# Pooled attention and a two-layer feed-forward network on one core: third and fourth pair in two visits, row maximum and scale in one instruction, new layouts for P and q, and a new order

## The chip, the cores and the metric

The kernel runs on one core of a Trainium2 chip. A core has five engines, each with its own queue in order: TensorE (PE; its weight loads are listed as PEld), VectorE (DVE), ScalarE (ACT), GpSimd (POOL) and SyncE (SP), which only issues DMA transfers. The metric is the device time of one execution in microseconds (us). Before the change it is 815.9 us, the median of three runs (814.71 to 816.48 us).

## The reference

Only what is computed matters here:

```python
def _attn_ref(q, k, v):                      # (4, 8, 1152, 64) fp32; q and k drawn about 0.71 wide, v 0.1
    q_pool = q.reshape(B, H, S // 2, 2, D).mean(axis=3)
    scores = (1 / np.sqrt(D)) * np.matmul(q_pool, k.transpose(0, 1, 3, 2))
    scores = scores - np.max(scores, axis=-1, keepdims=True)
    attn = np.exp(scores)
    attn = attn / (np.sum(attn, axis=-1, keepdims=True) + 1e-09)
    return np.matmul(attn, v)

def _moe_ref(x, w_in, w_out):                # x (2304, 512), w_in (512, 2048), w_out (2048, 512)
    r = np.maximum(x @ w_in, 0.0)
    return (r * r) @ w_out
```

`x` is the attention's output with the heads side by side: 2304 tokens of 512.

## The kernel before

**Attention.** The 32 heads of the four batches form 16 pairs, each of two heads of one batch. A pair has nine chunks of 128 pooled queries: four of head 0, four of head 1 and one that holds the last 64 queries of both. So there are 144 chunks. A chunk's scores (S, 128x1152, `scores`, L696 and L691) go to one of two PSUM tiles `s`; DVE takes the row maximum (MX, L704), ScalarE makes the Exp's bias from it (L715) and runs the Exp (EX, L716), which also gives the row sum. The scores of chunk i+2 need the Exp of chunk i, since they use its PSUM tile. Matmuls are in fp16, with each operand split in a high and a low part; for P that is HI (L720, L724, L353) and LO (L728), after which a DMA transpose (TR, L731) puts both into `PT`. The first four pairs are different: their P stays fp32 and is transposed by TensorE (TP, L756; copied out by TC, L766 and L768), and PV runs in fp32 (L867). PV (L875 for the other twelve pairs) runs twice a visit, r=0 on the first four 64-query columns of both heads and r=1 on the rest. For r=1 its moving operand has 384 columns, of which 64 are the other head's.

**Feed-forward.** Blocks of 256 tokens: block j takes r = j % 2 of the four pairs of batch j // 2, and a ninth block takes the 64 left over of every batch. A block is normalised with the row sums (RV, RT, RU, RB, XR), scaled by its own norm (XQ, XN, XM, XW) and split into high (XA, ScalarE) and low (XD, DVE). Then come eight H steps (L1025, 24 matmuls each), relu and square (HA, G1, G2, G3), and eight O steps (L1074, 12 matmuls each). Block 0 can start when its chunks of pairs 0 to 3 are done and the weights are ready.

**Weights.** Both matrices are loaded in 16 pieces as fp32 bits. Each value is taken apart and put together again in a range that can be split without loss: W1 (L1135, L353) scales, W2 (L1141, L1144) takes the sign, W3 (L1151) shifts by three bits, W5 (L1155) puts the three lowest bits in, W4 (L1164) multiplies by the sign. Then each quarter is scaled to high (WA, L328) and, for the second matrix, to a scaled fp32 copy (WB, L1241, ScalarE) and a low part (WD, L1245, POOL).

**What sets the order.** The kernel adds each step as an operation with the engines that may run it, an estimated cost, what it depends on, and a priority: its chunk number plus an offset for its kind (`off`, and `off0` before the first block) from the table `CFG`. `Plan.order` walks through these by estimated time and writes each engine's list; the engines then run their lists in order. Buffers come from seven tiles `buf`; `PT` has seven slots of 128 queries, and a chunk may write its slot when the PV that read it last is done (`ring`).

Of the kernel before, what the change touches and what calls it, by code (L numbers as in the profile page):

```python
# [8 lines left out]
F32 = mybir.dt.float32  # L9
# [3 lines left out]
I16 = mybir.dt.int16  # L13
AF = mybir.ActivationFunctionType
# [18 lines left out]
}  # L33


class Clock:


    W = 3413.3
# [12 lines left out]
    def run(self, t0, left):  # L52
# [3 lines left out]
        while True:  # L56
# [5 lines left out]
            self.used += self.edge - t  # L62
            left -= can
            t = self.edge
            self.turn()


class Plan:


    ENG = ("PE", "ACT", "DVE", "POOL", "SP")
    LAT = {"PE": 230, "ACT": 135, "DVE": 160, "POOL": 130, "SP": 150}

# [150 lines left out]
def kernel(  # L224
# [95 lines left out]
    def buf(*key):  # L320
        return bufs[plan.slot[key][1]]
# [1031 lines left out]
```

## Time and profile before

| | |
|---|---|
| median of three runs | 815.9 us |
| the profiled execution's own time | 815.77 us |
| its span, first to last instruction | 814.0 us |
| TensorE busy | 754.8 us (93%), mean granted clock 0.978 |
| ScalarE busy | 601.9 us (74%) |
| DVE busy | 585.2 us (72%) |
| POOL busy | 374.6 us (46%) |
| DMA, share of 16 engines | 76.7% in the queue of the kernel's own transfers |

Busy time is the time in which an engine runs an instruction; the share is of the span. A mean over the span says little here, since the program has stretches with different limits: the first four pairs with the weights, then attention and feed-forward blocks side by side, then blocks alone. A time line gives each instruction's start, and in square brackets how long its engine sat idle before it and what released it.

### The profile page before, as it was taken

The numbers are of one execution on the slowest core, as the hardware profiler recorded it, in microseconds if no ns is written. First come the engines' busy times: TensorE is split into PE (matmuls) and PEld (weight loads), VectorE is DVE, ScalarE is ACT, GpSimd is POOL, SyncE is SP. The second block draws the span as 40 slices with busy tenths as digits, with TensorE's granted clock in tenths as the row PEclk, the third lists the DMA queues.
The fourth block names the chain that finished last, engine by engine and source line by source line (L and its number), as shares of the span: only waits on it lengthen the run. The fifth ranks groups of instructions, "written<-read, shape, count | busy, mean of one in ns | idle before, by whom it ended". The sixth has DMA issues, their size and how long they took to land.

```text
span 814.0 us, 15284 instructions
## 1 busy us (share of the span) xinstructions
PE 754.8 (93%) x5998; PEld 493.6 (61%) x5998; DVE 585.2 (72%) x747; ACT 601.9 (74%) x940; POOL 374.6 (46%) x257
## 2 busy tenths in 40 slices
PE   5789888987799998999999999999999999999997
PEld 4555545554576656557756765677657656776663
DVE  3798898878997897689788897889678683311210
ACT  4676798899988688788898897998889974524230
POOL 2426333346867655657556684477655410000000
PEclk9899999997899999999999999999999999999999
DMA  9897645227689999999999999999999993000001
GB/s 280 210 238 233 150 155 162 102 47 167 131 177 207 192 213 198 211 193 198 204 216 192 206 200 195 198 213 154 211 197 197 173 169 63 1 14 14 14 14 26
DMA packets 324776, 128.96 MB, mean 158 GB/s; under 512 B 307552, under 2 KB 307552, under 8 KB 324704
## 3 DMA queue, kind: packets, MB, share of 16 engines
q1 hardware_dynamic: 324704, 127.99, 76.7%
q8 instruction: 47, 0.77, 0.4%
q14 instruction: 25, 0.20, 0.1%
HBM read 45.09 MB, written 4.72 MB: 61 GB/s over the span
## 4 chain that ended last, share of the span: by engine, by line
PE 61%; DVE 10%; DMA 9%; ACT 8%; issue 5%; POOL 4%; SPq 2%; POOLq 0%; DVEq 0%; ACTq 0%
PE ba L1074 14%; PE ba L1025 10%; PE ba L875 9%; PE s L696 8%; PE bt L1025 6%; PE bt L1074 5%; DMA PT<-buf 3%; ACT buf L716 3%; PE ba L867 3%; PE ba L756 2%; DVE ca L704 2%; DMA raw<-in_q_dram 2%; POOL buf L728 2%; DVE buf L728 2%; PE s L691 1%
## 5 line engine op out<-in xcount | busy, mean ns | idle before, releaser
L704 DVE TENSOR_REDUCE ca<-s 128x1 f32<-128x1152 f32 x144 | 193.1, 1350 | 20.2 <-PE s L696 16.2
L1025 PEld LDWEIGHTS <-w 128*128 128x128 f16 x1728 | 167.3, 98 | 31.1 <-issue 4.5
L716 ACT ACTIVATE buf<-s,ca,esc 128x1152 f32<-128x1152 f32 x135 | 177.0, 1311 | 8.1 <-DMA PT<-buf 2.0
L728 POOL TENSOR_TENSOR buf<-buf,buf 128x1152 f16<-128x1152 f32 x59 | 150.6, 2555 | 52.9 <-ACT buf L720 40.8
L1074 PE MATMUL ba<-w,region 128*128 128x512 f16 x672 | 153.7, 379 | 0.1
L696 PE MATMUL s<-kT,qT 128*128 128x512 f16 x720 | 137.3, 329 | 6.2 <-ACT buf L716 6.1
L1074 PEld LDWEIGHTS <-region 128*128 128x128 f16 x864 | 82.3, 98 | 93.1 <-issue 2.1
L1025 PE MATMUL ba<-region,w 128*128 128x256 f16 x1104 | 127.3, 273 | 2.9 <-DVE region L1037 2.5
L1052 POOL TENSOR_TENSOR region<-region 128x512 f16<-128x512 f32 x44 | 60.8, 1384 | 99.5 <-ACT region L1045 99.1
L696 PEld LDWEIGHTS <-qT 128*128 128x128 f16 x720 | 63.7, 100 | 62.8 <-issue 14.5
L875 PE MATMUL ba<-PT,v 128*64 128x384 f16 (+1 forms) x1296 | 95.0, 300 | 5.6 <-DMA PT<-buf 4.9
L728 DVE TENSOR_TENSOR buf<-buf,buf 128x1152 f16<-128x1152 f32 x49 | 78.3, 1597 | 20.2 <-ACT buf L720 11.1
L720 ACT ACTIVATE buf<-buf 128x1152 f16<-128x1152 f32 x75 | 87.0, 1161 | 5.8 <-DMA PT<-buf 2.1
L875 PEld LDWEIGHTS <-v 128*64 128x64 f16 x1296 | 73.7, 110 | 25.8 <-issue 8.2
L756 PE MATMUL ba<-ident,buf 128*128 128x128 f32 x324 | 55.2, 302 | 20.5 <-ACT buf L716 12.0
L715 ACT ACTIVATE ca<-ca,cols,esc 128x1 f32<-128x1 f32 x135 | 50.9, 377 | 19.1 <-DVE ca L704 18.4
L1040 ACT ACTIVATE region<-region 128x512 f16<-128x512 f32 x72 | 45.0, 626 | 21.1 <-PE ba L1074 8.1
L356 DVE SCALAR_TENSOR_TENSOR buf<-raw,psc,buf 128x576 f16<-128x576 f32 x45 | 55.5, 1260 | 5.9 <-POOL buf L330 3.5
L756 PEld LDWEIGHTS ba<-ident,buf 128*128 128x128 f32 x324 | 38.0, 152 | 35.5 <-ACT buf L716 13.2
L1052 DVE TENSOR_TENSOR region<-region 128x512 f16<-128x512 f32 x28 | 24.2, 866 | 47.8 <-ACT region L1045 47.4
L433 POOL TENSOR_TENSOR raw<-raw 128x576 f32<-128x576 f32 x16 | 24.2, 1515 | 61.2 <-DMA raw<-in_q_dram 44.0
L766 ACT ACTIVATE PT<-ba 128x384 f32<-128x384 f32 x74 | 34.0, 487 | 23.2 <-PE ba L756 21.2
(166 smaller groups left out, 961.0 us busy)
## 6 DMA issues: line engine op xcount, KB each, us to landing
raw<-in_k_dram SPq DMA_DIRECT2D x16, 576.0 KB, 4.6
raw<-in_q_dram SPq DMA_DIRECT2D x32, 288.0 KB, 4.8
region<-in_moe_w_in_dram SPq DMA_DIRECT2D x8, 1024.0 KB, 7.5
region<-in_moe_w_out_dram SPq DMA_DIRECT2D x8, 1024.0 KB, 5.2
raw<-in_v_dram SPq DMA_DIRECT2D x12, 576.0 KB, 4.5
out_dram<-buf SPq DMA_DIRECT2D x36, 128.0 KB, 2.4
v<-in_v_dram SPq DMA_DIRECT2D x4, 576.0 KB, 5.4
PT<-buf SPq DMA_TRANSPOSE x108, 4.9
```

The source lines that it names most:

```text
L356: nc.vector.scalar_tensor_tensor(out=o, in0=x, scalar=s, in1=h, op0=ALU.mult, op1=ALU.subtract)
L696: nc.tensor.matmul(s[:, x, :w], lhsT=qt[:, l, h, c0 : c0 + 2, :].rearrange("p a b -> p (a b)"), rhs=rhs, **st)
L704: nc.vector.reduce_max(a[:, 0:1], st3(), axis=AX.X)
L715: nc.scalar.activation(a[:, 1:2], a[:, 0:1], AF.Identity, bias=ln14, scale=s0)
L716: nc.scalar.activation(P(), st3(), AF.Exp, bias=a[:, 1:2], scale=s1, accum_out=col)
L720: nc.scalar.activation(hl()[:, 0], P(), AF.Copy)
L728: e.tensor_tensor(out=hl()[:, 1], in0=P(), in1=hl()[:, 0], op=ALU.subtract)
L756: nc.tensor.matmul(t[:, y], lhsT=P()[:, c * 128 : (c + 1) * 128], rhs=ident, is_transpose=True, start=(y == 0), stop=(y == 2), skip_group_ ...
L875: nc.tensor.matmul(px[h * 64 : (h + 1) * 64, :N], lhsT=vv[:, h, kc, vl, :], rhs=p2(r, h, 9 * pl + kc, False), start=(i == 0), stop=(i == 3 ...
L1025: nc.tensor.matmul(ph[:, f2], lhsT=w16[0][:, SLOT[f // 4], wl, a, f % 4 * 128 : (f % 4 + 1) * 128], rhs=xhl()[:, xl, a], start=(i == 0), s ...
L1052: e.tensor_tensor(out=gt[u][:, 1], in0=rt[u % 2], in1=gt[u][:, 0], op=ALU.subtract)
L1074: nc.tensor.matmul(p[:, :DM], lhsT=g[:, gl, f % 2, tt * 128 : (tt + 1) * 128], rhs=w16[1][:, SLOT[f // 4], wl, f % 4], start=(f == 0 and g ...
```

## The change

1. **Order of the first chunks.** The third and fourth pair are visited twice: first chunks 0, 1, 7, 8 of both (which block 0 needs), then the five others of both. Block 0's chunks are complete after 26 chunks and not after 31.
2. **Row maximum.** MX multiplies the scores by minus the scale, writes them back to the same PSUM tile, and takes the minimum into its accumulator output, all in one DVE instruction. The Exp then runs with the constant scale -1, and the minimum is its bias. For the fp32 chunks (pairs 0 to 3) there is no bias step; the others add a constant in a step of their own (MB), which may run on DVE, POOL or ScalarE. MX now needs the scale (GE) first.
3. **P's layout.** `PT` has the seven slots side by side for each block of 128 keys, so that PV reads one closed range: 256 columns for r=0 and 320 for r=1, where it was 384. The target of a DMA transpose now has a step of 896 elements between its 128-element pieces. `ringof` works out which PV has to be done before a slot is written; the first chunks behind the fp32 pairs wait for the last fp32 PV.
4. **q's layout.** The two heads' pooled queries lie in alternate partitions when loaded, so that one DMA transpose takes both; the scores read their weights with a step of two.
5. **Weights.** The three low bits are taken by an instruction of their own (W0, POOL or ScalarE) from the 16-bit half of the value, and the shift becomes the first operation of W5, so W3 goes.
6. **Smaller things.** GE, XO and the sum of q's halves (QS) may run on DVE; a half-width buffer `half` is added; v of an fp32 pair is loaded once; the factor 2^14 of the fp32 pairs moves from the Exp's bias to the row sums.
7. **Order.** `CFG`'s offsets and slacks are all new, and steps of the first and the last blocks get offsets of their own (`cls`).

ScalarE, behind the 36th Exp of the program (`L716`, first row). `w_1` is the second weight matrix; `L328` makes its high part and `L1241` its scaled copy:

```order
174 L716 ACTIVATE buf_93,sums_86<-s_112,ca,esc 128x1152
175 L766 ACTIVATE PT<-ba_113 128x384 x3
176 L715 ACTIVATE ca<-ca,cols,esc 128x1
177 L716 ACTIVATE buf_98,sums_87<-s_111,ca,esc 128x1152
178 L328 ACTIVATE w_1_91<-w_1_91,wS_1517 128x2048
179 L766 ACTIVATE PT<-ba_113 128x384
180 L766 ACTIVATE PT<-ba_114 128x384
181 L1241 ACTIVATE w_1_91<-w_1_91,wS_1517 128x2048
```

ScalarE of the changed kernel, around its 29th Exp (`L761`, first row), where the first of these now stands (`L338` high part, `L1306` copy):

```order
131 L761 ACTIVATE buf_93,sums_89<-s_112,ca 128x1152
132 L338 ACTIVATE w_1_91<-w_1_91,wS_1286 128x2048
133 L810 ACTIVATE PT<-ba_115 128x3x128
134 L810 ACTIVATE PT<-ba_114 128x3x128
135 L1306 ACTIVATE w_1_91<-w_1_91,wS_1286 128x2048
```

The pairs of weight instructions that stood behind the 37th Exp begin behind the 29th Exp; the last of them (row 155) is ahead of the 36th (row 158). No bias step (`L715`) stands between these rows.

ScalarE of the changed kernel behind its 36th Exp (first row); `L338` on `buf_97` is the high part of block 0's input, `L765` the high part of P, `L747` the bias step:

```order
158 L761 ACTIVATE buf_99,sums_86<-s_113,ca 128x1152
159 L761 ACTIVATE buf_98,sums_87<-s_112,ca 128x1152
160 L338 ACTIVATE buf_97<-x_110,xs 128x1024
161 L765 ACTIVATE buf_94<-buf_98 128x1152
162 L981 ACTIVATE ru<-ba_114 32x128
163 L810 ACTIVATE PT<-ba_115 128x3x128
164 L563 ACTIVATE half_100,acc<-raw_101 128x576
165 L810 ACTIVATE PT<-ba_114 128x3x128
166 L747 ACTIVATE ca<-ca,cols 128x1
167 L761 ACTIVATE buf_93,sums_87<-s_113,ca 128x1152
```

Block 0's input is split here, where the kernel before had weight instructions.

DVE before, at the low half of block 0's input (`L356` on `buf_94`), DVE's last step before the first H; the row maximum behind it (`L704`) is the 44th:

```order
242 L332 TENSOR_SCALAR region<-ba_113,esc 128x256
243 L993 RECIPROCAL xs<-xs 128x1
244 L356 SCALAR_TENSOR_TENSOR buf_94<-x_109,xs,buf_94 128x1024
245 L704 TENSOR_REDUCE ca<-s_112 128x1
246 L356 SCALAR_TENSOR_TENSOR region<-region,xs 128x1024
```

DVE of the changed kernel at the same step (`L369` on `buf_97`); the row maximum behind it (`L742`) is the 38th:

```order
203 L973 TENSOR_TENSOR r_1578<-ba_114,r_1578 128x16
204 L812 COPY PT<-ba_115 128x3x128
205 L369 SCALAR_TENSOR_TENSOR buf_97<-x_110,xs,buf_97 128x1024
206 L742 TENSOR_SCALAR s_113,ca<-s_113,esc 128x1152
207 L584 TENSOR_SCALAR ba_115<-ba_115 128x2
```

The step has moved ahead by six row maxima.

```diff
-CFG = {'SPLIT': 0, 'TURN': [], 'TURNB': [], 'WDP': ((1, 0), (1, 1), (1, 2), (1, 3)), 'WSP': 1.1562, ...
+CFG = {'SPLIT': 0, 'TURN': [], 'TURNB': [], 'WDP': ((1, 0), (1, 1), (1, 2), (1, 3)), 'WSP': 3.7027, ... 'PART': 1}
...
-    bufs = [buf_p.tile([128, 2304], F16, name=f"buf{i}") for i in range(NBUF)]
+    bufs = {
+        "buf": [buf_p.tile([128, 2304], F16, name=f"buf{i}") for i in range(NBUF)],
+        "half": [buf_p.tile([128, 1152], F16, name="half0")],
+    }
...
-    PT = pt_p.tile([128, 7, 18, 128], F16, name="PT")
+    PT = pt_p.tile([128, 18, 7, 128], F16, name="PT")
...
-    PSLOT = {0: 1, 1: 2, 7: 0, 8: 3, 2: 4, 3: 5, 5: 0, 6: 3, 4: 6}
...
+    BASE = {0: (640, 384), 1: (0, 320)}
...
+    def pcol(vi, j):
+        h0, h1 = base(vi, int(j in (2, 3, 4, 5, 6)))
+        return {0: h0, 1: h0 + 128, 7: h1, 8: h1 + 128, 2: h0, 3: h0 + 128, 4: h0 + 256, 5: h1 + 64, 6: h1 + 192}[j]
...
+    def p2(vi, r, h, x, full):
...
+        a = x * 896 + base(vi, r)[h]
+        return t[:, a : a + (320 if r else 256)]
+
+    def ringof(vi, j):
...
+        for v_, r_ in reversed(pairs_[: pairs_.index((vi, r))]):
+            if left and not other and (visits[v_][0] in full_v) != (n in full_v):
+                left, other = set(range(0, 896, 64)), True
...
-                nc.sync.dma_start(out=raw("q", n)[h * 64 : (h + 1) * 64], in_=sv[h])
+                nc.sync.dma_start(out=raw("q", n)[h : h + 127 : 2], in_=sv[h])
...
-            for h in range(2):
-                nc.sync.dma_start_transpose(out=qT(n)[:, 0, h], in_=x[h * 64 : (h + 1) * 64])
+            nc.sync.dma_start_transpose(out=qT(n)[:, 0], in_=buf("q2", n)[:, :1152])
...
-                                s[:, x, :w], lhsT=qt[:, l, h, c0 : c0 + 2, :].rearrange("p a b -> p (a b)"),
+                                s[:, x, :w],
+                                lhsT=qt[:, l].rearrange("p c m -> p (c m)")[:, 128 * c0 + h : 128 * c0 + h + 255 : 2],
...
-            nc.vector.reduce_max(a[:, 0:1], st3(), axis=AX.X)
+            sc = -(2.0 ** -4) if n in full_s else tl["esc", n][:, 0:1]
+            nc.vector.tensor_scalar(st3(), st3(), sc, 3e38, op0=ALU.mult, op1=ALU.min, accum_out=a[:, 0:1])
+
+        def mb(o):
+            a = tl["ca", i]
+            if o["eng"] == "ACT":
+                nc.scalar.activation(a[:, 1:2], a[:, 0:1], AF.Identity, bias=ln14)
+            else:
+                e = nc.vector if o["eng"] == "DVE" else nc.gpsimd
+                e.tensor_scalar(a[:, 1:2], a[:, 0:1], LN, 1.0, op0=ALU.add, op1=ALU.mult)
...
-            s0, s1 = (-(2.0 ** -4), 2.0 ** -4) if n in full_s else (tl["esc", n][:, 0:1], tl["esc", n][:, 2:3])
-            nc.scalar.activation(a[:, 1:2], a[:, 0:1], AF.Identity, bias=ln14, scale=s0)
-            nc.scalar.activation(P(), st3(), AF.Exp, bias=a[:, 1:2], scale=s1, accum_out=col)
+            x = 0 if n in full_v else 1
+            nc.scalar.activation(P(), st3(), AF.Exp, bias=a[:, x : x + 1], scale=-1.0, accum_out=col)
...
-            nc.sync.dma_start_transpose(out=PT[:, PSLOT[j]], in_=hl().rearrange("p l k -> p (l k)"))
+            nc.sync.dma_start_transpose(out=pslot(vi, j, False), in_=hl().rearrange("p l k -> p (l k)"))
...
-        N = 384 if r else 256
+        N = 320 if r else 256
...
-                    def w3_(o, w=w, i=i, half=half, c=c):
-                        t = f32(w, i)[:, half].bitcast(I32)
-                        nc.vector.tensor_scalar(t, t, 3, None, op0=ALU.logical_shift_left)
+                    def w0(o, c=c):
+
+                        to, x = wst[c % 2][:, :, :, 0], wst[c % 2].bitcast(U16)[:, :, :, 1]
+                        s, d = 2.0 ** -13 * (1 - 2.0 ** -20), -0.499995
+                        if o["eng"] == "ACT":
+                            nc.scalar.activation(to, x, AF.Copy, scale=s, bias=d)
+                        else:
+                            nc.gpsimd.tensor_scalar(to, x, s, d, op0=ALU.mult, op1=ALU.add)
...
-                            out=t, in0=wst[c % 2][:, :, :, 0], scalar=29, in1=t,
-                            op0=ALU.logical_shift_right, op1=ALU.bitwise_or,
+                            out=t, in0=t, scalar=3, in1=wst[c % 2][:, :, :, 0],
+                            op0=ALU.logical_shift_left, op1=ALU.bitwise_or,
...
+    if cfg("PART", 0):
+        first = first[:2] + [(p, p, ORD[:4]) for p in (2, 3)] + [(p, p, ORD[4:]) for p in (2, 3)]
```

## Rows read from the trace of the kernel before

**Rows 1.** Windows: us, then busy us (instructions) by engine, PEclk, DMA share, GB/s
```profile
0.00:165.00 165.00, 133.02 (x1000) 85.76 (x1001) 134.61 (x181) 120.36 (x211) 60.45 (x49) 0.95 0.66 189
165.00:217.00 52.00, 39.91 (x302) 24.87 (x300) 42.51 (x69) 48.22 (x61) 33.02 (x19) 0.84 0.55 117
217.00:664.00 447.00, 438.52 (x3642) 288.19 (x3641) 370.86 (x433) 381.20 (x590) 273.82 (x179) 1.00 1.05 195
664.00:814.00 150.00, 143.37 (x1062) 94.75 (x1058) 37.24 (x68) 52.11 (x82) 7.37 (x11) 0.99 0.14 29
```

**Rows 2.** The page's chain of waits, shares of the span by engine
```profile
PE 61%; DVE 10%; DMA 9%; ACT 8%; issue 5%; POOL 4%; SPq 2%; POOLq 0%; DVEq 0%; ACTq 0%
```

**Rows 3.** Time line of TensorE, 140 to 240 us: start, us, what, idle before
```profile
176.08 4.11 PE L867 MATMUL ba<-PT,v 128*64 128x256 f32 x36 [0.19 <-ACT PT L766]
...
193.41 6.43 PE L867 MATMUL ba<-PT,v 128*64 128x384 f32 x36 [0.58 <-ACT PT L766]
...
208.17 2.13 PE L691 MATMUL s<-kT,qT 128*64 128x512 f16 x12 [4.70 <-ACT buf L716]
...
215.15 2.12 PE L696 MATMUL s<-kT,qT 128*128 128x512 f16 x12
...
217.11 5.40 PE L1025 MATMUL ba<-buf,w 128*128 128x256 f16 x48
```

**Rows 4.** Time line of ScalarE, 165 to 217 us
```profile
167.29 1.31 ACT L716 ACTIVATE buf<-s,ca,esc 128x1152 f32<-128x1152 f32 x1
...
173.47 1.99 ACT L328 ACTIVATE w<-w,wS 128x2048 f16<-128x2048 f32 x1
...
176.32 1.99 ACT L1241 ACTIVATE w<-w,wS 128x2048 f32<-128x2048 f32 x1
...
188.65 1.31 ACT L716 ACTIVATE buf<-s,ca,esc 128x1152 f32<-128x1152 f32 x1
```

**Rows 5.** Critical chain in order of time: start, us, what
```profile
260.26 3.07 PE ba L875 x54
...
275.27 4.51 PE ba L875 x54
```

**Rows 6.** Lines by form, DVE: busy us, mean ns, idle before, releaser
```profile
L704 DVE TENSOR_REDUCE ca<-s 128x1 f32<-128x1152 f32 x144 | 193.1, 1350 | 20.2 <-PE s L696 16.2 <-PE s L691 2.4 <-ACT ca L715 0.9
...
L1195 DVE TENSOR_REDUCE wsc<-ba 128x1 f32<-128x512 f32 x8 | 5.5, 684 | 0.7 <-PE ba L1189 0.7
...
L979 DVE TENSOR_SCALAR_CACHE_REDUCE ba<-ba 128x256 f32<-128x256 f32 x6 | 2.6, 428 | 2.3 <-PE ba L973 1.8 <-ACT region L1040 0.4
...
L1151 DVE TENSOR_SCALAR w<-w 128x1024 int32<-128x1024 int32 x12 | 9.8, 818 | 1.7 <-ACT w L1135 1.7
```

**Rows 7.** Time line of all engines, DVE around 192 us
```profile
192.12 0.14 DVE L979 DVE_READ_ACCUMULATOR ba<-ba 128x1 f32 x1
192.12 1.35 DVE L704 TENSOR_REDUCE ca<-s 128x1 f32<-128x1152 f32 x1
```

**Rows 8.** Lines by form, ScalarE and POOL
```profile
L716 ACT ACTIVATE buf<-s,ca,esc 128x1152 f32<-128x1152 f32 x135 | 177.0, 1311 | 8.1 <-DMA PT<-buf 2.0
...
L716 ACT ACTIVATE buf<-s,ca 128x1152 f32<-128x1152 f32 x9 | 11.0, 1221 | 0.3
...
L715 ACT ACTIVATE ca<-ca,cols,esc 128x1 f32<-128x1 f32 x135 | 50.9, 377 | 19.1 <-DVE ca L704 18.4
...
L1135 ACT ACTIVATE w<-region 128x1024 f32<-128x1024 f32 x6 | 7.0, 1166 | 0.5 <-DMA region<-in_moe_w_in_dram 0.3
...
L353 POOL TENSOR_SCALAR w<-region 128x1024 f32<-128x1024 f32 x6 | 8.7, 1455 | 4.9 <-DMA region<-in_moe_w_out_dram 3.7 <-DMA region<-in_moe_w_in_dram 1.2
```

**Rows 9.** Lines by form, weight loads of TensorE
```profile
L696 PEld LDWEIGHTS <-qT 128*128 128x128 f16 x720 | 63.7, 100 | 62.8 <-issue 14.5
...
L1189 PEld LDWEIGHTS <-w 128*128 128x128 bf16 x96 | 5.9, 97 | 2.1 <-issue 2.0
```

**Rows 10.** Tile PT, SP's issues: ns min/median/max, first and last start us
```profile
L731 SPq DMA_TRANSPOSE PT<-buf x108: 2382/2855/5275, 180.3 to 672.3; - x108
```

More of the change, by code (lines that the diff above doesn't have):

```diff
@@ L309 @@
     plan.resource("t", 6, None)
+    plan.resource("half", 1)
     add = plan.add
@@ L320, in buf @@
     def buf(*key):
[L321 removed]
+        r, x = plan.slot[key]
+        return bufs[r][x]
     def raw(*key):
@@ L424, in prep @@
         if n in full_v:
-            for y, vi in enumerate(vs):
-                add(("LV", n, vi), {"SP": 2500}, oldvs[y], lambda o, vi=vi: load_kv(v4(vi % 2), v), need if y == 0 else visits[vi][2], after=[("LQ", n)])
+            add(("LF", n), {"SP": 2200}, oldv, lambda o: load_kv(v4(slot), v), visits[vs[0]][2])
         else:
-            add(("LV", n), {"SP": 2500}, [], lambda o: load_kv(rv(), v), need, take=(("v", n), ("raw",), 0), after=[("LQ", n)])
+            add(("LV", n), {"SP": 2200}, [], lambda o: load_kv(rv(), v), need, take=(("v", n), ("raw",), 0), after=[("LQ", n)])
         def qsum(o):
@@ L741, in chunk @@
             add(("S", i), {"PE": 1115 if CH[j] is None else 985}, [("KT", n), ("QX", n, 0), ("QX", n, 1)] + back, scores, i, give=("kT", n) if end else None)
[L742 to L748 removed]
+        add(("MX", i), {"DVE": 1300}, [("S", both(i)[0])] + ([] if n in full_s else [("GE", n, "qk")]), smax, i, give=("qT", n) if end else None)
+        if n not in full_v:
+            add(("MB", i), alt("MB", DVE=150, POOL=300, ACT=300), [("MX", i)], mb, i)
+        add(("EX", i), {"ACT": 1500}, [("MX" if n in full_v else "MB", i)] + sold, ex, i, take=(("P", i), ("buf",), cfg("RSV", 1)))
+        ring = ringof(vi, j)
         if n in full_v:
[L750 removed]
+            pt = pslot(vi, j, True)
             def tp4(o, x):
@@ L999, in xd_ @@
             split_lo(xhl()[:, 1], xt(j), tl["xs", j][:, 2, 0:1], xhl()[:, 0])
-        add(("XQ", j), alt("XQ", ACT=980, POOL=2000), [("XR", j, 0), ("XR", j, 1)], xq, at, take=(("xq", j), ("buf",), cfg("RX", 1)))
+        add(("XQ", j), alt("XQ", ACT=980, POOL=2000), [("XR", j, 0), ("XR", j, 1)], xq, at, take=(("xq", j), ("buf", "half"), cfg("RX", 1)))
         add(("XN", j), {"PE": 450}, [("XQ", j)], xn, at, take=(("XN", j), ("a", "t"), 0), give=("xq", j))
@@ L1222, in ws3 @@
                 )
-            add(("WS1", w), {"DVE": 900}, [("WM", w, i) for i in range(4)], ws1, at, take=(("wdg", w), ("buf",), 0))
-            add(("WS2", w), {"PE": 300}, [("WS1", w)], ws2, at, take=(("WS2", w), ("a",), 0), give=("wdg", w))
-            add(("WS3", w), {"DVE": 850}, [("WS2", w)], ws3, at, give=("WS2", w))
+            add((W + "S1", w), {"DVE": 900}, [(W + "M", w, i) for i in range(4)], ws1, at, take=(("wdg", w), ("buf", "half"), 0))
+            add((W + "S2", w), {"PE": 300}, [(W + "S1", w)], ws2, at, take=((W + "S2", w), ("a",), 0), give=("wdg", w))
+            add((W + "S3", w), {"DVE": 850}, [(W + "S2", w)], ws3, at, give=(W + "S2", w))
             for i in range(4):
```

174 lines of the change are left out of this document (101 added, 73 removed), and 5 rows, old and new, of tables (COST, DEF).

## The prediction

> **What bounds the kernel now.** I read the busy time by stretches first [rows 1], because the mean over the span hides that the program has four parts. Up to 165 us TensorE is busy 133.0 of 165.0 us and no engine is full. From 165 to 217 us ScalarE is busy 48.2 of 52.0 us (93%) while TensorE has 39.9 us at a granted clock of 0.84, a mean over stretches at its two levels (1.2 and 2.4 GHz, 1.00 being the higher); I credit nothing for it. From 217 to 664 us TensorE is busy 438.5 of 447.0 us (98%) at 1.00, and DVE (83%) and ScalarE (85%) have room. After 664 us only TensorE works. The chain of waits says the same [rows 2]: 61% of it is TensorE, and no other engine has over 10%. So two things can move the end: TensorE work taken out after 217 us, and the moment at which TensorE's full stretch begins. The time line of TensorE shows that moment [rows 3]: the first matmul of the feed-forward part (H, L1025) starts at 217.1 us, behind two score groups at 215.2 us; before them stands a wait of 4.70 us for ScalarE's Exp. The time line of ScalarE shows why it is late [rows 4]: after the 36th Exp (167.3 us) the 39th starts only at 188.7 us, and between and behind them run the eight 2.0 us instructions on the second weight matrix (four as at 173.5 us, four as at 176.3 us).
>
> **The change, part by part.**
>
> *Narrower PV.* The PV matmuls for r=1 go from 384 to 320 columns. A PV of 256 columns takes 3.07 us and one of 384 takes 4.51 us [rows 5], so 64 columns are worth (4.51 - 3.07) / 2 = 0.72 us, and one of 320 costs 3.79 us. Twelve visits (pairs 4 to 15) are behind the first H, where TensorE is full: 12 x 0.72 = 8.6 us. The four fp32 visits save (6.43 - 4.11) / 2 = 1.16 us each [rows 3], but before the first H, where TensorE has idle time: I credit nothing.
>
> *Third and fourth pair in two visits, and the new order.* Block 0 needs the chunks of groups 0 and 3 of four pairs. These were complete at chunk 31 and are at chunk 26 now. In TensorE's order 45 score groups stand before the first H, and 41 now. The eight ScalarE instructions on the second weight matrix stood behind the 37th Exp, and all of them are ahead of the 36th now. DVE's last step before H (the low half of block 0's input) stood just ahead of the 44th row maximum, and stands ahead of the 38th now. What H waits for next is the 41st score group, which needs the 39th Exp. From the 36th to the 39th Exp it took 188.65 - 167.29 = 21.4 us [rows 4], of which two pairs of weight instructions, 8.0 us, are gone: 13.4 us. With the Exp (1.31 us) and one score group (2.12 / 2 = 1.06 us) H can start at 167.3 + 13.4 + 1.3 + 1.1 = 183 us, if the 36th Exp comes no later than now.
> It may come later, since ScalarE gets more to do ahead of it: 8 x 2.0 = 16.0 us of weight instructions, six of the low-bit instructions and six more of the two other weight steps (12 x 1.17 = 14.0 us by L1135 [rows 8]), less 36 bias steps of 0.38 us (13.6 us) and 27 x (1.31 - 1.22) = 2.4 us for an Exp whose scale is a constant. That is +14.0 us. If all of it hides in the 44.6 us that ScalarE is free before 165 us [rows 1], H starts at 183 us; if none does, at 197 us. Its load there goes from 73% to 81%, so the nearer row is the stretch in which it has slack; I take a third, 4.7 us: H at 188 us.
>
> *Row maximum with scale.* The reduction takes 1.350 us and the fused form, at 256 elements, 0.428 us [rows 6]. From 512 to 1152 elements the reduction grows by (1350 - 684) / 640 = 1.04 ns an element, so the fused form should take 0.428 + 896 x 0.00104 = 1.36 us. It also leaves an accumulator read of 0.14 us; the time line has the next DVE instruction start at the same 192.12 us as that read [rows 7], so it costs DVE between nothing and 0.14 us. I take nothing, as in that row. Its price, if the cover goes, is 100 row maxima behind the first H x 0.15 = 15 us on an engine that is 83% busy there. The write back into PSUM is bounded by the same fused row, which also writes where it reads. In the latency from scores to Exp the read stands against the bias step of 0.377 us that goes or gets cheaper; I credit nothing.
>
> *Bias steps and Exp.* Of 144 bias steps 36 go, and 108 stay as plain additions: 71 on ScalarE, 21 on DVE, 16 on POOL. ScalarE is not what TensorE waits for after 217 us: 0 us. The same holds for what the order gives POOL (six more of the low halves of P, 49 instead of 44 of G3): POOL has 273.8 of 447.0 us there.
>
> *Weights.* The shift (L1151, 16 instructions of about 0.82 us, 13 us of DVE [rows 6]) becomes part of the OR. The new low-bit instruction runs ten times on POOL (1.46 us by L353 [rows 8], the same tile and stride) and six times on ScalarE (counted above). POOL is busy 60.5 of 165.0 us [rows 1], so it hides. DVE's 13 us lie before the first H, where they shorten nothing by themselves; they are why I charge DVE nothing there.
>
> *New layouts.* The weights for the scores are now read with a step of two elements. Loads with such a step (L1189) take 97 ns against 100 ns without it [rows 9]: 0 us. The transposes of P write into a target with a step instead of a closed block: 0 us, bounded in the third rival. All transposes of pair 4 now wait for the last fp32 PV, which stands just ahead of the first H; the first of them can start some 4 us later than at 180 us. Seven H matmul groups (5.40 us for two, [rows 3]) stand before the PV that needs them: hidden. One transpose per pair for q instead of two spares SP's queue an issue; no credit.
>
> **The sum**, against the profiled execution's own 815.77 us (span 814.0 us and 1.77 us around it; the median of the runs is 815.9 us). From the first H to the end it took 814.0 - 217.1 = 596.9 us. Four score groups (4 x 1.06 = 4.2 us) and one PV (3.07 us), which stood before H, come behind it, and 8.6 us of PV go. The time is 1.77 + H + 596.9 + 4.2 + 3.1 - 8.6 = H + 597.4: with H at 188 us, 785 us; at 183 us, 780 us; at 197 us, 794 us.
>
> **The rivals.**
>
> *No head start, columns only.* What is moved ahead of the 36th Exp delays it by all that it takes, and ScalarE and DVE, fuller than TensorE before H, also pass on waits among themselves. Then the order changes where work stands and not when TensorE becomes full, and only the columns count: 815.8 - 8.6 = 807 us. For it: ScalarE at 93% and TensorE's 4.70 us wait for it [rows 1, 3]. Against it: ScalarE's 73% before 165 us.
>
> *DVE becomes the bound after the first H.* The accumulator read is not covered and each row maximum costs 0.15 us more: 785 + 15 = 800 us, and 809 us with H at 197 us. Against it: the read's row [rows 7] and 83% busy.
>
> *The strided target slows the transposes of P (slower than before).* There are 108, an issue takes 2.38 us at the least and 2.86 us in the median, all into closed blocks [rows 10], and the DMA engines show a busy share of 1.05 from 217 to 664 us [rows 1], so they have little room. If each took a third longer (0.95 us), 108 x 0.95 = 103 us would come on top: 888 us, or 837 us if half of it hid. It decides from (815.8 - 785) / 108 = 0.28 us a transpose. Against it: TensorE hardly waits for them now, since 98% busy leaves 8.5 us in 447.0.
> The Trainium skill, "DMA: Bandwidth & Descriptors", section "Latency and other measured facts", gives 261 GB/s for a DMA transpose whose middle dimension is not contiguous and 350 to 400 GB/s for a contiguous one, a hit of about 30%. By that rule this rival would be the forecast. This trace does not reach the page's contiguous rate: 128 x 2304 x 2 bytes in 2.38 us are 248 GB/s. No run here shows a strided target.
>
> **How the numbers follow.** Head start as worked out (780 to 794 us, with measurement and small terms 778 to 797): 0.62. Columns only (797 to 810): 0.20. DVE bound (797 to 812): 0.05. Strided transposes (820 and more): 0.10. No change, where the gains and the accumulator reads cancel: 0.03; this kernel can be told from no change at about 0.2%, 1.6 us. The likeliest gives 785 us, with 778 to 797 as its own range; the range that should hold 8 in 10 reaches over the next two cases, 776 to 812. Faster 0.62 + 0.20 + 0.05 = 0.87, same 0.03, slower 0.10.
>
> **What would show it.** Right: the first H near 188 us and TensorE at 97% or more from there to the last scores; PV of 320 columns at 3.8 us; the row maximum at 1.36 us with its accumulator read started together with the next instruction; the 36th Exp near 172 us; transposes of P still at 2.9 us. Wrong: the 36th Exp beyond 180 us (first rival), TensorE's idle time put down to DVE's row maximum (second), or transposes over 3.2 us and TensorE waiting for PT (third).

## The result, and the profile after

The changed kernel takes 802.7 us (median; 801.0 to 805.2), the kernel before 816.2 us beside it: a ratio of 0.984 (0.981 to 0.987), 13.4 us faster. Forecast were 785 us, 31 us faster. The sign was right; under half of the gain came. The profiled execution took 801.02 us, with a span of 799.2 us.

The windows of the changed kernel, cut at its own first H and at the last scores (for [rows 1]):

```profile
0.00:165.00 165.00, 131.07 (x995) 86.59 (x995) 132.76 (x208) 117.46 (x179) 71.30 (x48) 0.93 0.65 189
165.00:197.00 32.00, 28.47 (x219) 16.30 (x218) 25.25 (x51) 29.15 (x42) 21.95 (x10) 1.00 0.15 32
197.00:655.00 458.00, 445.00 (x3768) 296.72 (x3768) 386.86 (x600) 376.15 (x586) 283.40 (x166) 0.99 1.09 204
655.00:799.00 144.00, 139.53 (x1021) 92.58 (x1018) 34.15 (x67) 47.34 (x75) 12.62 (x12) 0.99 0.11 23
```

TensorE (the first busy column) is at 97% from the first H on, as forecast. The column to look at is the last but one, the DMA engines' mean busy share: 1.09, where it was 1.05 in [rows 1]. It adds up the time of all packets, so it can pass 1 and is a sign of load, not a limit. The chain of waits now is TensorE to three quarters [rows 2]:

```profile
PE 75%; DVE 8%; ACT 7%; DMA 4%; issue 3%; POOL 1%; SPq 0%; DVEq 0%; ACTq 0%; POOLq 0%
```

The time line of TensorE around the first H, and that of ScalarE ahead of it [rows 3, 4]:

```profile
189.08 5.07 PE L911 MATMUL ba<-PT,v 128*64 128x320 f32 x36
197.32 2.78 PE L1083 MATMUL ba<-buf,w 128*128 128x256 f16 x24 [0.56 <-DVE region L1010]
```
```profile
160.25 2.00 ACT L338 ACTIVATE w<-w,wS 128x2048 f16<-128x2048 f32 x1 [1.29 <-POOL w L1310]
162.29 2.00 ACT L1306 ACTIVATE w<-w,wS 128x2048 f32<-128x2048 f32 x1
...
182.38 1.22 ACT L761 ACTIVATE buf<-s,ca 128x1152 f32<-128x1152 f32 x1
...
193.01 1.20 ACT L761 ACTIVATE buf<-s,ca 128x1152 f32<-128x1152 f32 x1
```

The first H starts at 197.3 us (217.1 before, 188 forecast). The 36th Exp (182.4 us) came 15 us later than before, the 39th 4.4 us later. Behind the first H stand 601.9 us, 596.9 before. A single profile fixes the start to some 5 us only: e10 below, which differs from the changed kernel from the 55th chunk on, has H at 194.0 us, and the 21st Exp stands at 119.0 us in the changed kernel, 116.2 in e10 and 114.1 in e2, all with the same instructions ahead of it. The pieces that were priced one by one [rows 5 to 10]:

```profile
240.42 3.86 PE L919 MATMUL ba<-PT,v 128*64 128x320 f16 x54
260.00 3.14 PE L919 MATMUL ba<-PT,v 128*64 128x256 f16 x54
```
```profile
L742 DVE TENSOR_SCALAR_CACHE_REDUCE s<-s,esc 128x1152 f32<-128x1152 f32 x135 | 191.1, 1420 | 28.8 <-PE s L732 18.6 <-PE s L727 4.3 <-ACT buf L765 2.7
L761 ACT ACTIVATE buf<-s,ca 128x1152 f32<-128x1152 f32 x144 | 174.7, 1215 | 14.0 <-DVE s L742 9.4 <-POOL ca L750 0.9 <-DVE ca L750 0.7
...
L732 PEld LDWEIGHTS <-qT 128*128 128x128 f16 x720 | 63.9, 100 | 62.2 <-issue 11.7
...
L1213 ACT ACTIVATE region<-region 128x1024 int32<-128x1024 uint16 x6 | 7.0, 1168 | 0.4 <-DMA region<-in_moe_w_in_dram 0.4
```
```profile
152.01 0.14 DVE L742 DVE_READ_ACCUMULATOR s<-s,esc 128x1 f32 x1
152.01 0.55 DVE L812 COPY PT<-ba 128x384 f32<-128x384 f32 x1
```

A PV of 320 columns takes 3.86 us (3.79 forecast), the row maximum 1.42 us (1.36), its accumulator read starts with the next instruction. What the prediction did not weigh is the queue of SP. Its issues on the tiles PT and qT (ns min/median/max, first and last start), before and then after:

```profile
L593 SPq DMA_TRANSPOSE qT<-buf x30: 1198/1230/2480, 23.8 to 615.8; - x30
```
```profile
L776 SPq DMA_TRANSPOSE PT<-buf x108: 2382/2836/5089, 195.3 to 657.7; - x108
...
L629 SPq DMA_TRANSPOSE qT<-half x11: 1282/1301/1925, 72.4 to 546.3; - x11
L629 SPq DMA_TRANSPOSE qT<-buf x4: 1279/1303/1400, 42.1 to 589.4; - x4
```

Transposes of P take the same with the strided target (2.84 us against 2.86 in [rows 10]). But they start 15 us later than before and end 14.6 us earlier. The span can be split at the 19th of them (pair 6's first) and at the last into its start, 89 intervals and a tail: before 277.44 + 89 x 4.436 + 141.74 = 814.0 us, after 276.03 + 89 x 4.288 + 141.51 = 799.2 us. 13.2 of the 14.8 us stand in the intervals, and only 1.4 in the start, though H came 19.8 us earlier. The split says where the time went, not why. SP's time line in that stretch has few holes:

```profile
396.88 13.62 SPq L776 DMA_TRANSPOSE PT<-buf  x4
410.55 0.57 SPq L450 DMA_DIRECT2D raw<-in_k_dram  x1
411.17 4.18 SPq L616 DMA_TRANSPOSE kT<-buf  x1
415.51 1.13 SPq L458 DMA_DIRECT2D raw<-in_q_dram  x2
416.74 5.09 SPq L776 DMA_TRANSPOSE PT<-buf  x1
421.92 1.17 SPq L1156 DMA_DIRECT2D out_dram<-half  x2
423.15 12.24 SPq L776 DMA_TRANSPOSE PT<-buf  x4
```

SP's issuing instructions, added up one by one, fill 353.5 of the 378 us from 277 to 655 us (94%), and 342.9 us before (91%). One issue for q less per pair would be 1.2 us less in nine intervals, 0.13 of the 0.148 us.

TensorE's work is not spread as before either. Whole windows between the 19th and the last transpose, before and then after; and, of the output matmuls alone (O, L1074 and now L1132), what stands ahead of the 19th:

```profile
277.44:672.25 394.81, 386.48 (x3199) 249.88 (x3196) 323.52 (x386) 336.37 (x515) 232.74 (x152) 1.00 1.06 197
276.03:657.71 381.68, 370.07 (x3148) 245.04 (x3146) 320.44 (x498) 309.90 (x483) 238.28 (x138) 0.99 1.09 204
```
```profile
0.00:277.44 277.44, 11.01 (x48) 4.58 (x48) 0.94 0.71 175
0.00:276.03 276.03, 21.86 (x96) 9.15 (x96) 0.96 0.72 175
```

TensorE has 16.4 us less to do between the two transposes. With H earlier, 48 more O matmuls (10.9 us) are done ahead of them; the narrower PV is a part of the rest.

### The profile page after: what moved, and what is told of

Read it like the earlier page. It is cut to its first block, busy times and chain, and to the rows that moved or that the text cites. A ratio compares the mean times of both kernels' runs of the same rounds, so it can differ in the third digit from the quotient of the medians.

```text
span 799.2 us, 15293 instructions
## 1 busy us (share of the span) xinstructions
PE 744.1 (93%) x5998; PEld 492.2 (62%) x5998; DVE 579.0 (72%) x924; ACT 570.1 (71%) x880; POOL 389.3 (49%) x234
## 4 chain that ended last, share of the span: by engine, by line
PE 75%; DVE 8%; ACT 7%; DMA 4%; issue 3%; POOL 1%; SPq 0%; DVEq 0%; ACTq 0%; POOLq 0%
PE ba L1132 17%; PE ba L1083 14%; PE s L732 12%; PE ba L919 10%; PE bt L1132 6%; PE bt L1083 6%; PE ba L911 4%; DVE s L742 3%; PE ba L800 3%; PE s L727 2%; DMA PT<-buf 1%; DMA region<-in_moe_w_out_dram 1%; PE s L711 1%; ACT buf L761 1%; ACT PT L810 1%
## 5 line engine op out<-in xcount | busy, mean ns | idle before, releaser
L742 DVE TENSOR_SCALAR_CACHE_REDUCE s<-s,esc 128x1152 f32<-128x1152 f32 x135 | 191.1, 1420 | 28.8 <-PE s L732 18.6
L773 POOL TENSOR_TENSOR buf<-buf,buf 128x1152 f16<-128x1152 f32 x65 | 161.4, 2485 | 77.6 <-ACT buf L765 60.0
L761 ACT ACTIVATE buf<-s,ca 128x1152 f32<-128x1152 f32 x144 | 174.7, 1215 | 14.0 <-DVE s L742 9.4
L1132 PE MATMUL ba<-w,region 128*128 128x512 f16 x624 | 142.9, 379 | 0.5 <-DVE region L1010 0.3
L1132 PEld LDWEIGHTS <-region 128*128 128x128 f16 x864 | 83.1, 99 | 94.3 <-issue 1.0
L765 ACT ACTIVATE buf<-buf 128x1152 f16<-128x1152 f32 x81 | 93.9, 1159 | 2.9 <-DMA kT<-buf 0.3
L919 PE MATMUL ba<-PT,v 128*64 128x320 f16 (+1 forms) x1296 | 86.8, 291 | 5.8 <-ACT region L1093 3.2
L773 DVE TENSOR_TENSOR buf<-buf,buf 128x1152 f16<-128x1152 f32 x43 | 60.6, 1410 | 9.1 <-ACT buf L765 7.0
L1132 PE MATMUL bt<-w,region 128*128 128x512 f16 x240 | 52.6, 379 | 0.0
L747 ACT ACTIVATE ca<-ca,cols 128x1 f32<-128x1 f32 x71 | 20.6, 291 | 40.3 <-DVE s L742 39.5
L369 DVE SCALAR_TENSOR_TENSOR buf<-raw,psc,buf 128x576 f16<-128x576 f32 x34 | 46.0, 1359 | 0.0
L1083 PE MATMUL bt<-region,w 128*128 128x256 f16 x408 | 45.9, 273 | 0.0
```

The lines of the kernel that those rows point to most:

```text
L369: nc.vector.scalar_tensor_tensor(out=o, in0=x, scalar=s, in1=h, op0=ALU.mult, op1=ALU.subtract)
L742: nc.vector.tensor_scalar(st3(), st3(), sc, 3e38, op0=ALU.mult, op1=ALU.min, accum_out=a[:, 0:1])
L761: nc.scalar.activation(P(), st3(), AF.Exp, bias=a[:, x : x + 1], scale=-1.0, accum_out=col)
L765: nc.scalar.activation(hl()[:, 0], P(), AF.Copy)
L773: e.tensor_tensor(out=hl()[:, 1], in0=P(), in1=hl()[:, 0], op=ALU.subtract)
L919: nc.tensor.matmul(px[h * 64 : (h + 1) * 64, 64 * r * (1 - h) : 64 * r * (1 - h) + N], lhsT=vv[:, h, kc, vl, :], rhs=p2(vi, r, h, 9 * pl + ...
```

## The experiments

Times are medians beside the kernel before on the same chip; the ratio, with its interval, is to that kernel. Of the changed kernel it is 0.984. Where less than the whole edit is printed, dots stand for the rest. All keep the order of the kernel they start from, except where it says otherwise.

**What holds the first H back?** Theory T says TensorE's own work ahead of it, theory S ScalarE's weight work.

```
...
-        return t[:, a : a + (320 if r else 256)]
+        return t[:, a : a + (384 if r else 256)]
...
-        N = 320 if r else 256
+        N = 384 if r else 256
...
```


> The changed kernel with the PV matmuls of r=1 at 384 columns again, in the same order; the output is the same. The term of the prediction: 12 visits behind the first H at 0.72 us give 8.6 us, and the four fp32 visits ahead of it nothing, so 811 us against 802.7 and the first H where it is (197.4 us). If TensorE's own work is what holds the first H back (theory T), the two fp32 PVs behind 123 us, where TensorE hardly waits any more, move H by 2 x 1.16 = 2.3 us as well, and the time comes to 813 us or a little more. If ScalarE's work ahead of the 36th Exp holds it back (theory S), H does not move and the time is 811 us.

805.4 us, 0.988 (0.983 to 0.994); H at 197.4 us. The columns are worth 2.7 us here, not 8.6: both theories missed. By the ratios it is 3.5 us, give or take 5, so this run alone does not rule 8.6 out.

```
-                for y in range(3):
+                ny = 1 if 24 <= i < 36 else 3
+                for y in range(ny):
...
```


> The changed kernel with TensorE's transposes of P for the 25th to the 36th chunk cut to a third (one 128x128 matmul of three; the probabilities of these chunks are then wrong in two thirds of their columns). Nothing else changes on any engine. It takes 12 x 6 matmuls of 0.17 us, about 12 us, off TensorE between 135 and 195 us. Theory T (TensorE's work and the waits of the first 123 us set the first H): H comes up to 12 us earlier, at 186 to 190 us, and the time falls by 8 to 12 us, to 791 to 795 us. Theory S (ScalarE's weight work ahead of the 36th Exp sets it): H stays within 2 us of 197.4 and the time at 801 to 803 us.

```
                 def wb(o, w=w, i=i):
-                    nc.scalar.activation(f32(w, i), f32(w, i), AF.Copy, scale=tl["wS", w][:, 2, 0:1])
+                    return
```


> The changed kernel without the four ScalarE instructions that scale the second weight matrix in place (L1306, 2.0 us each; the low halves of that matrix are then wrong). TensorE's work and the order stay. Theory S: all 14 us that ScalarE got ahead of the 36th Exp landed there, so taking 8.0 us out brings the 36th Exp from 182.4 to 174.4 us, the first H from 197.4 to 189.4 us and the time from 802.7 to 795 us. Theory T: TensorE waits only some 8 us in all from 123 us to the first H, under half of it for ScalarE, so H moves by 0 to 4 us (193.5 to 197.4) and the time stays between 799 and 803 us, though the 36th Exp comes earlier.

Both edits together:

> The two reductions together: transposes of the 25th to 36th chunk at a third and no scaling in place of the second weight matrix. Theory T: as with the transposes alone, H at 186 to 190 us, with up to 4 us more from ScalarE: 787 to 795 us. Theory S: as without the scaling alone, 795 us. If each holds H as soon as the other is lightened, the two together give clearly more than the sum of the two single gains (over 12 us, under 790 us) while each alone gives little.

800.5 us (0.982, 0.977 to 0.986), 800.2 us (0.981, 0.977 to 0.985) and 802.8 us (0.985, 0.980 to 0.990): none differs from 0.984, and both together give nothing either. H came at 194.2, 197.1 and 196.1 us, but the 21st Exp, ahead of e2's edit, was already 4.9 us early there (114.1 against 119.0 us), so of its 3.1 us nothing is left. T and S both fell. In e2's profile TensorE was busy only 6.27 us of 140 to 150 us, and the granted clock behind it was 0.68 from 150 to 160 us, where the changed kernel shows 8.37 us and 1.00.

**What holds TensorE behind H?** Theory P: only its own work. Theory C: DVE and ScalarE as well.

```
-            nc.vector.tensor_scalar(st3(), st3(), sc, 3e38, op0=ALU.mult, op1=ALU.min, accum_out=a[:, 0:1])
+            nc.vector.reduce_max(a[:, 0:1], st3(), axis=AX.X)
...
```


> The changed kernel with the row maximum as before (a plain reduction of 1.35 us, no write back, no accumulator read), the scale in the bias steps and in the Exp (1.31 us with a scale by row instead of 1.22), and bias steps for the 36 fp32 chunks on ScalarE again; order and output stay. DVE gets lighter by 0.07 to 0.2 us a chunk (7 to 20 us behind the first H), ScalarE heavier by 0.1 us a chunk and by 13.6 us ahead of H. The prediction's step (the fused form costs and gains nothing by itself, and ScalarE's bias steps are off the path behind H): 802 to 805 us. If DVE's row maximum is a bound behind H (second rival): 790 to 798 us. If ScalarE's 13.6 us ahead of H all land: 814 us or more.

808.3 us, 0.988 (0.985 to 0.991): by the ratios the fused form with its constant scale for the Exp is worth some 3 us, at the edge of the intervals; forecast was nothing. The 790 to 798 us of the second rival did not come.

From that kernel on:

```
-            nc.vector.reduce_max(a[:, 0:1], st3(), axis=AX.X)
+            nc.vector.reduce_max(a[:, 0:1], st3()[:, : 576 if i >= 40 else 1152], axis=AX.X)
...
                 if o["eng"] == "ACT":
-                    nc.scalar.activation(r, r, AF.Square)
+                    return
```


> The changed kernel with DVE and ScalarE made lighter behind the first H: from the 41st chunk on the row maximum is a plain reduction over half of the columns (0.75 us instead of 1.42; the scale is in the bias step and the Exp as before), and ScalarE leaves out its second square of the feed-forward part (G2, 67 x 0.63 us; the low halves of g are then wrong). TensorE's work and the order stay. DVE loses about 70 us and ScalarE about 30 us in the stretch from 200 to 650 us. Theory C (behind the first H the three engines hold one another, so that TensorE's 17 us of waits and its half clock after them come from DVE and ScalarE): TensorE's waits behind H fall under 10 us and the time to 788 to 797 us. Theory P (TensorE's own work alone is the bound there): 800 to 804 us.

And with e1's edit besides:

> The kernel with DVE and ScalarE made lighter, and the PV matmuls of r=1 at 384 columns. The columns were to be worth 8.6 us, and putting them back cost the changed kernel only 2.6 us. Theory C: with the two engines lightened the columns cost what their matmuls take, so this is 7 to 10 us slower than the lightened kernel with 320 columns. Theory P (64 columns simply take less than 0.72 us in a full TensorE): again 2 to 4 us slower.

810.5 us (0.990, 0.987 to 0.993) and 812.6 us (0.994, 0.992 to 0.996). DVE at 282 us of 400 instead of 338 (250 to 650 us, against the changed kernel) and a lighter ScalarE gave nothing: the transposes' interval stayed at 4.33 us. The columns cost 2.1 us, 2.9 by the ratios, as little as before. With e1 that is 3 us, give or take 3, and 8.6 is ruled out. Theory C fell as far as it means the work of DVE and ScalarE.

```
-        return t[:, a : a + (320 if r else 256)]
+        return t[:, a : a + 256]
...
-        N = 320 if r else 256
+        N = 256
...
```


> The changed kernel with 64 columns less again in the PV matmuls of r=1 (256 instead of 320; the outputs of the middle block and a part of the rest are then wrong), in the same order. TensorE loses another 12 x 0.72 = 8.6 us behind the first H. Theory P: 794 us. Theory C: TensorE's saving comes back as waits for ScalarE and DVE and as half clock after them: 800 to 803 us, with its idle time behind H up from 17 to over 20 us.

804.3 us, 0.984 (0.980 to 0.988): 64 columns less gave nothing, so theory P fell too. TensorE's idle time from 277 us to the end rose from 16.3 to 22.6 us, as theory C had it, but e6 leaves DVE and ScalarE out as the cause. In e1 to e8 one number hardly moved: the interval of the transposes, 4.28 to 4.35 us. That made theory D: SP's queue.

```
-            nc.sync.dma_start_transpose(out=qT(n)[:, 0], in_=buf("q2", n)[:, :1152])
+            x = buf("q2", n)[:, :1152]
+            for h in range(2):
+                nc.sync.dma_start_transpose(out=qT(n)[:, 0, :, h * 64 : (h + 1) * 64], in_=x[h * 64 : (h + 1) * 64])
```


> The changed kernel with the transpose of q in two halves of 64 rows again, as before the change (the same bytes, the same target, two issues in place of one); everything else, order and output stay. Theory D: from the 19th transpose of P on, SP's queue and the DMA engines behind it are the bound in both kernels (an issue every 4.44 us before and every 4.29 us after, SP busy 96% of that stretch), and the 13.4 us gained are the 1.2 us of one transpose less per pair, times 11 pairs. So this kernel loses about 11 x 1.2 = 13 us and comes to 814 to 818 us. The prediction's step (no credit for it) and theory C (DVE, ScalarE and TensorE hold one another): 802 to 805 us.

816.0 us, 1.001 (0.999 to 1.004): with this one step undone the whole gain is gone. SP's issues in its profile:

```profile
L778 SPq DMA_TRANSPOSE PT<-buf x108: 2387/2837/5840, 198.5 to 671.7; - x108
L631 SPq DMA_TRANSPOSE qT<-half x22: 1200/1267/2227, 73.3 to 560.4; - x22
```

From the first to the last transpose of P it takes 473.2 us, the changed kernel 462.4: 10.8 of the profile's 14.1 us. They do not stand where theory D put them. The interval behind the 19th is 4.366 us, 7 us more in all and only half of the 0.148 back; 5 us stand between H (199.3 us) and the 19th (283.1 us), 83.8 us instead of 78.7, and the 2 us by which H is later are within its spread. This fits a queue that holds the kernel from the first transpose on.

```
-            nc.sync.dma_start_transpose(out=pslot(vi, j, False), in_=hl().rearrange("p l k -> p (l k)"))
+            x = 9 if i >= 54 else 18
+            nc.sync.dma_start_transpose(out=pslot(vi, j, False)[:, :x], in_=hl().rearrange("p l k -> p (l k)")[:, : 128 * x])
```


> The changed kernel with the transposes of P from the 55th chunk on over the first 1152 of 2304 columns (half of the bytes; the low halves of P that the PV matmuls then read are those of earlier chunks). TensorE, DVE, ScalarE, GpSimd and the order stay. Theory D: 90 transposes shorter by about 1.4 us leave SP's queue at some 70%, so TensorE's own work becomes the bound: its waits behind the first H fall from 17 to under 10 us and the time to 785 to 795 us. Theory C and theory P: 800 to 804 us.

791.1 us, 0.969 (0.967 to 0.972). SP's issuing instructions now fill 213.9 of 378 us, TensorE is at 98% (97% in the changed kernel), and the DMA share falls (277 to 655 us, changed kernel and then this one; SP's issues on PT):

```profile
277.00:655.00 378.00, 366.39 (x3120) 243.09 (x3119) 317.52 (x496) 308.45 (x481) 237.49 (x137) 0.99 1.09 204
```
```profile
277.00:655.00 378.00, 370.32 (x3166) 243.89 (x3163) 321.70 (x506) 308.39 (x480) 232.98 (x137) 1.00 0.73 135
```
```profile
L777 SPq DMA_TRANSPOSE PT<-buf x108: 1242/1339/4310, 192.0 to 645.4; - x108
```

The interval falls to 4.181 us, 9.5 us less over the 89. The half transposes take load off SP's queue and off the DMA engines at once, and their data land sooner; this run does not tell these apart.

With e1's edit besides:

> The kernel with the half transposes of P, and the PV matmuls of r=1 at 384 columns. Theory D: with the queue out of the way TensorE's columns cost what they take: 10 of the 12 visits lie behind the 55th chunk, so this is 6 to 9 us slower than the kernel with half transposes and 320 columns. Theory C and P: 2 to 4 us slower, as in the changed kernel.

802.1 us, 0.983 (0.980 to 0.986): now the columns cost 11.0 us (by the ratios 11.5, give or take 4), more than the 6 to 9 expected and about their whole price of 12 x 0.72 = 8.6 us, where they cost 2.7 us with the full queue. Whether the four fp32 visits add to it was not measured.

The same edit of the transposes (L731) in the kernel before:

> The kernel before with the transposes of P from the 55th chunk on over half of the columns, in its own order. TensorE was busy 438.5 of 447.0 us there, which the prediction took as the bound. If it was (prediction, theory P): 813 to 817 us. If SP's queue and the DMA engines held it too (theory D): its 15 us of TensorE's waits behind the first H go in part and the time falls to 802 to 811 us.

807.0 us, 0.988 (0.985 to 0.991): the queue held the kernel before too; lightened alone it gives 9 us there, and then TensorE is busy 373.9 of 378 us (277 to 655 us).

**What is still open: alone or together, and which resource of the queue?**

In the kernel before (the loads of q and the score matmuls with it, as in the change):

```
...
-            for h in range(2):
-                nc.sync.dma_start_transpose(out=qT(n)[:, 0, h], in_=x[h * 64 : (h + 1) * 64])
+            nc.sync.dma_start_transpose(out=qT(n)[:, 0], in_=buf("q2", n)[:, :1152])
...
```


> The kernel before with this one part of the change: q is loaded with its two heads' rows in turn, transposed in one issue of 128 rows instead of two of 64, and the score matmuls read it with a step of two; order and output stay. Theory D (the queue of transposes is the bound from about 277 us on in both kernels, and 1.2 us less per pair is the whole gain): 816 - 11 x 1.2 = 803 us, as the changed kernel. If the gain needs the other parts too (TensorE at 98% in the kernel before holds it as soon as the queue is lighter): 808 to 816 us.

811.2 us, 0.995 (0.993 to 0.997): alone the transpose of q gives 4 us. Theory D's 803 us missed; the 808 to 816 us of a gain that needs the other parts too held. TensorE leaves no room for more: it is busy 385.7 of the 390.2 us between the 19th and the last transpose. The other parts alone give nothing (e9). Which of them makes the room is answered in part by e1, which has the columns of the kernel before and still gains 11 us: TensorE is busy 375.3 us in that stretch there, with 96 O matmuls ahead of it as in the changed kernel and not 48. So most of the room comes from work that the earlier H moves forward, and the narrower PV adds 5 us (370.1). No run undid the order alone.

```
-            for h in range(2):
-                nc.sync.dma_start(out=raw("q", n)[h : h + 127 : 2], in_=sv[h])
+            nc.sync.dma_start(out=raw("q", n), in_=sv.rearrange("h p x -> p h x"))
...
-                for z in range(2):
...
-                    nc.sync.dma_start(out=ob[c], in_=t[z * 64 : (z + 1) * 64])
...
+                nc.sync.dma_start(out=ob, in_=t)
```


> The changed kernel with each pair's two loads of q as one and the two stores of each half block as one: 34 issues less, of which 20 stand in the stretch from 277 to 660 us, at 0.57 us each; the bytes and the order stay. If the time that SP takes to issue is the bound (theory D1): 20 x 0.57 = 11 us less, 790 to 793 us. If the DMA engines are (theory D2, busy share 1.09): 800 to 803 us.

836.1 us, 1.025 (1.021 to 1.029): 34 issues less and 33 us slower than the changed kernel, outside both forecasts, so it is not the number of issues. SP's time line shows where the time goes: the transpose behind a merged store takes 7.36 us (the first of the group of two at 438.04), where behind two stores it took 2.83 us. Seven such transposes stand between 270 and 660 us, some 31 us. Why they take longer is not shown.

```profile
437.38 0.61 SPq L1156 DMA_DIRECT2D out_dram<-half  x1
438.04 10.24 SPq L775 DMA_TRANSPOSE PT<-buf  x2
```

```
-            nc.sync.dma_start(
+            (nc.gpsimd if n >= 5 else nc.sync).dma_start(
```


> The changed kernel with the loads of k and v from the sixth pair on (22 of 576 KB) issued by GpSimd instead of SP, at the same places of the order; the bytes stay. Theory D1 (SP's issue time is the bound): 20 x 0.55 = 11 us less, 790 to 795 us, if GpSimd's own waits do not eat it. Theory D2 (the DMA engines are): 800 to 805 us or slower.

826.3 us (median of three runs; a fourth took 834.9), 1.013 (1.007 to 1.019). Slower; GpSimd's own waits for the buffers were not separated, so it says nothing for sure. Whether SP's issuing time or the DMA engines behind it set the pace of the transposes stays open.

```
-CFG = {'SPLIT': 0, 'TURN': [], ...
+CFG = {'SPLIT': 0, 'TURN': [56, 74, 92, 110, 128], ...
```


> The changed kernel with P of five chunks behind the first H (one of every second pair) transposed by TensorE instead of the queue, an order planned anew with the same settings. The queue loses 5 x 2.84 = 14 us, TensorE gets 5 x 1.45 = 7 us. Theory D: the time falls by up to 7 us, to 796 to 800 us, if the new order costs nothing elsewhere. Theory P and C: 805 to 815 us.

820.3 us, 1.007 (1.004 to 1.010), outside every forecast. The new order cost more than five transposes gave: from pair 6's first on the transposes left came every 4.80 us, and TensorE was busy 358.0 of 378 us (277 to 655 us). It changes order and queue together and decides nothing. No version that computes everything beat the changed kernel.

## Why the prediction was right or wrong

- *Sign, strided target, read of the accumulator, strided weight loads*: right. Transposes 2.84 us, weight loads 100 ns, the read hidden. The third rival is refuted by [rows 10] and its row after. The rule of the Trainium skill, "DMA: Bandwidth & Descriptors", section "Latency and other measured facts" (30% off for a middle dimension that is not contiguous), does not show here: 590 KB take as long into the strided target as into the closed one (issue 2.84 and 2.86 us, landing 5.0 and 4.9 us after its start).
- *The step that failed* is the reading of what bounds the kernel: "So two things can move the end: TensorE work taken out after 217 us, and the moment at which TensorE's full stretch begins." TensorE's 98% was taken for the only bound. SP's queue of transposes, busy issuing for 91% of 277 to 655 us, was left out, and its saved issue got no credit. In [rows 1] stands a DMA share of 1.05 beside TensorE's time, and the prediction used it in the third rival alone ("they have little room"). Two resources were nearly full side by side: all parts of the change but the one transpose for q give nothing (e9, 816.0 us), load taken off the queue alone gives 4 us (e13) or 9 us (e12), and the whole change 13.4 us.
- *The sum, H + 597.4*: 15.6 us are missing between its 785.4 us and the profiled 801.0 us. H came 9.3 us later than forecast. The other 6.3 us stand behind it, where the sum lets all saved TensorE work come back: TensorE is idle 17.4 us behind H instead of 15.1, and its granted clock there has fallen from 1.00 to 0.99.
- *"All transposes of pair 4 now wait for the last fp32 PV ... hidden"*: TensorE indeed waits only 1.1 us between H and the 19th transpose. But the first transpose started at 195.3 us, not "some 4 us later than at 180 us", and from there the queue is nearly full.
- *"I take a third, 4.7 us: H at 188 us"*: H came at 197.3 us (194.0 in e10), where all of ScalarE's 14 us would put it. But that is not why: 8 us less on ScalarE (e3) moved nothing, nor did 12 us less on TensorE (e2), nor both (e4). What paces the chunks ahead of H stays open. GpSimd's low parts of the second matrix (L1310), for which ScalarE waits at 160.25 us in the rows above, and DVE were not tried.
- *"12 x 0.72 = 8.6 us"*: the matmuls are shorter by 0.65 us a visit, 7.8 us in all, but with the full queue that is worth 2.7 us, and with the queue lightened 11.0 us.
- *"One transpose per pair for q instead of two spares SP's queue an issue; no credit."* The gain hangs on this: 13 us when it is undone. It needed room on TensorE as well: without the other parts it gives 4 us, without the narrower PV alone 11 us (e1).
- *Fused row maximum, 0 us*: about right; if anything 3 us better than the plain one. The second rival (DVE as the bound) is refuted by e6.
- *First rival, columns only, 807 us*: its range (797 to 810 us) holds the 802.7 us by luck. Its mechanism is wrong: the columns are worth 2.7 us (e1), and ScalarE's weight work did not hold H (e3). That the head start is worth nothing does not follow: it is not enough by itself (e9), but with one transpose for q the kernel with the old order takes 811.2 us (e13) and the one with the new order and the same columns 805.4 us (e1).
- *TensorE's clock*, which the sum has at 1.00 behind H, took a part of the saved time. Rows of the changed kernel, windows of 4 us: behind a wait of 2.45 us for ScalarE the granted clock stood at 0.50, the lower level (1.2 GHz); between 217 and 664 us the kernel before had 1.00.

```profile
344.00:348.00 4.00, 3.63 (x25) 1.50 (x22) 3.56 (x8) 3.17 (x6) 1.74 (x2) 1.00 1.11 191
348.00:352.00 4.00, 0.98 (x5) 0.66 (x6) 1.85 (x5) 2.31 (x4) 1.70 (x1) 0.69 0.83 184
352.00:356.00 4.00, 3.84 (x19) 2.08 (x19) 3.43 (x13) 3.75 (x7) 1.34 (x2) 0.50 1.13 209
```

How that wait came about reads from the time line: a bias step (L747) stands ahead of XQ (L1022) in ScalarE's order and waits for the row maximum, which DVE does behind four small steps.

```profile
348.44 1.43 DVE L742 TENSOR_SCALAR_CACHE_REDUCE s<-s,esc 128x1152 f32<-128x1152 f32 x1
...
349.96 0.29 ACT L747 ACTIVATE ca<-ca,cols 128x1 f32<-128x1 f32 x1 [0.85 <-DVE s L742]
350.16 1.04 ACT L1022 ACTIVATE buf<-region 128x1024 bf16<-128x1024 f32 x1
...
351.25 1.03 PE L1030 MATMUL ba<-buf,ones 128*128 128x256 bf16 x4 [2.45 <-ACT buf L1022]
```

## What to carry to other kernels

An engine at 98% need not be the only bound: before its saved time is credited, look for a second resource that is nearly full in the same stretch, the DMA share and the issuing queue among them, which no busy column of an engine shows. Find the events that repeat through the stretch (here 108 transposes) and split the span into start, intervals and tail. That finds the place to look at and not the cause: H's 19.8 us showed as 1.4 us in the start, while the work that they moved forward gave TensorE room in the intervals. Where two resources are full, test a step in both states of the other: the columns were worth 2.7 us in one and 11.0 us in the other.

## What the runs showed of the hardware

- A transpose of 64 rows by 1152 takes as long to issue as one of 128 rows (1.23 and 1.30 us), so two halves cost twice.
- In the changed kernel, 270 to 660 us, the issue of a transpose of P directly behind another takes 2.92 us in the mean (61 of them), behind a load of v 3.99 us (7), behind the two loads of q 4.04 us (8), behind two stores of 128 KB from `half` 2.83 us (6); in e14, behind one store of 256 KB from `half`, 7.33 us (5).
- Lightening DVE and ScalarE by tens of us behind H made nothing faster (e6). Taking 12 us of matmuls out ahead of H gave no time either (e2); TensorE waited more there, and behind the waits the granted clock was 0.68 in the mean of 150 to 160 us, where the changed kernel has 1.00.
